# Three of the weights' low parts subtracted on GpSimd instead of being made by TensorE

## The chip, the cores and the metric

The kernel runs on one core of a Trainium2 chip. Its engines are TensorE (PE, with its weight loads shown as PEld), VectorE (DVE), ScalarE (ACT), GpSimd (POOL) and SyncE (SP), which issues the loads and stores. The metric is the device time of one execution in microseconds, the median of several runs.

## What is computed

The reference has two halves. The first is attention with local and global keys, for 4 batches of 8 heads, 768 positions and head dimension 64; the second is a channel mix of the result with its predecessor in the sequence:

```python
scores = scale * q @ k.T + bias        # bias = -slope(head) * distance
scores = where(is_global | is_local, scores, -1e9)   # 8 global keys, 96 local
x = softmax(scores) @ v                # then [B, S, 512]
x_prev = concatenate([0, x[:, :-1]], axis=1)
xk = mu_k * x + (1 - mu_k) * x_prev
xr = mu_r * x + (1 - mu_r) * x_prev
k = maximum(xk @ w_k, 0)               # w_k [512, 1024]
v = k * k @ w_v                        # w_v [1024, 512]
out = sigmoid(xr @ w_r) * v            # w_r [512, 512]
```

The three weights come as 64-bit floats.

## The kernel before

The 4 x 768 positions are cut into 24 tiles of 128. For every tile and pair of heads PE makes the scores (`s_n_hp`, lines 357 and 358 in the first eight tiles), DVE adds the bias and takes the maximum (L366), ACT exponentiates (L367), DVE takes the reciprocal of the sum (`r_n_hp`, L373 and L374), and of each four heads three are scaled by `r` on POOL (L380) and one on ACT (L378). PE transposes the scaled heads (`t_n_hp`, L392), ACT copies them out of PSUM (`et`), and PE multiplies them by the values (`av_n`, L411). A scaled head is called `e_n_h`.

Two tiles make a chunk of 256 positions for the channel mix. `mix` makes `xk` and `xr` (L435 or L437 for the predecessor's part, L438 on DVE) and cuts each into a high part on ACT (L439, type fp32r) and a low part on DVE (L440, `xk_lo` and `xr_lo`). Each product is then three matmuls: high by high, high by low, low by high (L447 to L449). `kp` are the products of `xk` with w_k, `z` those of `xr` with w_r, `vps` those of the square with w_v. In the `kp` products the weight is the stationary operand: line 447 is its high part by `xk_hi`, line 448 its high part by `xk_lo`, line 449 its low part by `xk_hi`.

The weights are cut the same way. They lie in DRAM as 64-bit words and come in ten blocks of 1 MB: 0 to 3 are w_k (`wk0` to `wk3`), 4 and 5 are w_r (`wr0`, `wr1`), 6 to 9 are w_v (`wv0` to `wv3`). A block's words land in `w64_i`. `weight_begin` makes a 32-bit float `wa_i` of them in three steps on DVE (L174, L175, L176) and its high part on ACT (L178). `weight_end` makes the low part: for w_k and w_r through PE, which puts `wa` times the identity less the high part into a PSUM tile `rest` (L188 and L189, in two halves of 512 columns; L188 is a product of 32-bit floats and has two records in the trace for each instruction), from which ACT casts it (L190); for w_v directly on DVE by a subtraction of 128 x 1024 (L192).

W_BEGUN says at which point of the program a block is begun; it is ended one such point later. A scheduler that times the program by its own estimates then sets the order in which the instructions of all engines stand; each engine works through its own list in that order and waits for what the instruction at its head needs. The conversion of the weights, the first tiles' attention and the first chunk's `kp` lie in the first 100 us; afterwards the weights stay in SBUF.

Of the kernel before, what the change touches and what calls it, by code (L numbers as in the profile page):

```python
# [9 lines left out]
F32 = mybir.dt.float32  # L10
# [22 lines left out]

W_LOADS = (2, 2, 2, 2, 3, 3, 4, 4, 4, 5, 5, 6, 6, 7, 7, 8, 8, 9, 9, 10)
W_BEGUN = (1, 1, 2, 2, 3, 3, 4, 4, 4, 5, 5, 6, 6, 6, 7, 7, 8, 8, 9, 9, 10)
GAP = {"kk_hi": 16, "xk_lo": 112}
FAR = 1.0e12
HUGE = (1.875 - 2.0**-13) * 2.0**32
# [3 lines left out]
def tile_biased_attention_channel_mix(ctx: ExitStack, tc: tile.TileContext, qT, kT, v, n_sizes, mu_kr, w_k, w_v, w_r, q_rows, k_rows, v_rows, slopes, out):  # L42
    nc = tc.nc
    vec, act, pool, pe = nc.vector, nc.scalar, nc.gpsimd, nc.tensor
# [57 lines left out]
    f_pool.tile([128, 96], F32, name="ahead", tag="ahead")  # L102
    btmp = f_pool.tile([128, 2048 + GAP["kk_hi"]], F32, name="btmp", tag="kk_hi")
    cut = iter((0, 352, 704, 928, 1056, 1184, 1184 + W))
# [77 lines left out]
    def weight_end(i):  # L182
        name, src, j = w_steps[i]
        a, both = w_live.pop(i)
        if name in 'kr':
            for o in (0, 512):
                rest = ps_f.tile([128, 512], F32, name=f"rest_{i}_{o}", tag="f")
                pe.matmul(rest, ident, a.bitcast(F32)[:, o : o + 512], start=True, stop=False)  # L188
                pe.matmul(rest, minus, both[:, 0, o : o + 512], start=False, stop=True)  # L189
                act.copy(both[:, 1, o : o + 512], rest)  # L190
        else:
            vec.tensor_sub(both[:, 1, :], a.bitcast(F32), both[:, 0, :])  # L192
        for k in range(1 if name == "k" else 2):
            kn = both if name == "k" else both[:, :, k * 512 : (k + 1) * 512]
            wts[name, j if name == "k" else 2 * j + k] = kn[:, 0, :], kn[:, 1, :]
# [41 lines left out]
    def weights_load(n):  # L237
        while w_count[2] < min(n, len(w_steps)):
            weight_load(w_count[2])
            w_count[2] += 1  # L240

    def weights_go(begun, ended):
        weights_load(begun)
        while w_count[0] < min(begun, len(w_steps)):
            weight_begin(w_count[0])
            w_count[0] += 1
        while w_count[1] < min(ended, w_count[0]):
            weight_end(w_count[1])
            w_count[1] += 1
# [175 lines left out]
    def part(pool, tag, n):  # L425
        t = pool.tile([128, n * 256 + GAP.get(tag, 0)], F32R, name=tag, tag=tag)
        return t[:, 0 : n * 256].rearrange("p (a q) -> p a q", a=n)
# [97 lines left out]
    for step in range(NTILES + 1):  # L525
# [6 lines left out]
        for hp in range(4):  # L532
# [19 lines left out]
            weights_load(W_LOADS[min(slot, len(W_LOADS) - 1)])  # L552
            n = W_BEGUN[min(slot, len(W_BEGUN) - 1)]
            weights_go(n, n - 1 if slot < len(W_BEGUN) else n)
    for i in range(4):
# [190 lines left out]
```

## Time and profile before

| | |
|---|---|
| median of 3 runs | 509.49 us (509.43 to 509.81) |
| the profiled execution | 509.01 us, its span 507.2 us |
| busy in the span | PE 98%, DVE 68%, ACT 68%, POOL 44% |
| granted TensorE clock, mean | 0.996 of full speed |
| waits of PE after 20 us | 1.2 us, the first L448 for `xk_lo` |

The profile is of one execution; the span runs from its first to its last instruction, and 1.8 us lie around it. The busy shares are means over the whole span, and what holds in the first 100 us, where the change is, is read from the windows and timelines of that stretch.

### The profile page before, as it was taken

How to read it: one execution, taken by the hardware profiler on the slowest of the kernel's cores; microseconds unless marked ns; L12 is line 12 of the kernel's file. 1: busy time of each engine (PE TensorE's matmuls, PEld its weight loads, DVE VectorE, ACT ScalarE, POOL GpSimd, SP SyncE). 2: the span in 40 equal slices, each digit the busy share in tenths (PEclk: the TensorE clock that was granted, in tenths of full speed). 3: DMA queues.
4: the chain of work that ended last, by engine and by line, in shares of the span. 5: the costliest groups of instructions: out<-in, count | busy, mean ns of one | idle time of the engine just before them, and what ended most of it. 6: DMA issues, size and time to landing. Idle time of an engine off the chain costs nothing. (4 is left out here: it accounts for less than half of the span.)

```text
span 507.2 us, 10304 instructions
## 1 busy us (share of the span) xinstructions
PE 495.6 (98%) x3600; PEld 434.4 (86%) x3600; DVE 342.9 (68%) x837; ACT 345.0 (68%) x857; POOL 221.5 (44%) x368
## 2 busy tenths in 40 slices
PE   6999999999999999999999999999999999999995
PEld 3767898998898898898898898898898898897984
DVE  6986988466388768658768758748768755457441
ACT  4889789567467668667577677667577678587360
POOL 8631435224448445527447536428438435204000
PEclk9999999999999999999999999999999999999999
DMA  8998331503913433513513513513423215647311
GB/s 242 323 241 241 137 111 51 151 1 101 209 34 80 107 100 79 151 55 80 142 46 81 149 57 80 142 64 79 124 66 81 82 40 163 208 156 258 126 41 48
DMA packets 24234, 59.95 MB, mean 118 GB/s; under 512 B 5328, under 2 KB 6352, under 8 KB 23664
## 3 DMA queue, kind: packets, MB, share of 16 engines
q1 hardware_dynamic: 24032, 59.23, 40.6%
q8 instruction: 30, 0.49, 0.4%
q14 instruction: 28, 0.23, 0.2%
q10 hardware_dynamic: 144, 0.00, 0.0%
HBM read 52.93 MB, written 6.29 MB: 117 GB/s over the span
## 5 line engine op out<-in xcount | busy, mean ns | idle before, releaser
L380 POOL TENSOR_SCALAR e<-e,r 128x232 f32<-128x232 f32 (+1 forms) x180 | 89.2, 514 | 162.2 <-DVE r L374 125.4
L447 PE MATMUL kp<-xk_hi,wk 128*128 128x256 f32 x384 | 108.8, 283 | 0.0
L448 PE MATMUL kp<-xk_lo,wk 128*128 128x256 f32 x384 | 107.5, 280 | 1.2 <-DVE xk_lo L440 1.2
L367 ACT ACTIVATE e<-e,nmax 128x232 f32<-128x232 f32 (+1 forms) x192 | 89.9, 471 | 26.5 <-DVE nmax L366 25.8
L449 PE MATMUL kp<-xk_hi,wk 128*128 128x256 f32 x384 | 107.5, 280 | 0.0
L366 DVE CUSTOM_DVE_ANT_0 e<-s,pat 128x232 f32<-128x232 f32 (+1 forms) x192 | 64.7, 373 | 25.2 <-PE s L361 14.0
L447 PE MATMUL vps<-wv,kk_hi 128*128 128x512 f32 x192 | 75.6, 395 | 0.0
L449 PE MATMUL vps<-wv,kk_lo 128*128 128x512 f32 x192 | 75.2, 392 | 0.0
L448 PE MATMUL vps<-wv,kk_hi 128*128 128x512 f32 x192 | 75.0, 391 | 0.0
L448 PEld LDWEIGHTS kp<-xk_lo,wk 128*128 128x128 f32 x384 | 72.1, 188 | 2.0 <-DVE xk_lo L440 1.4
L447 PEld LDWEIGHTS kp<-xk_hi,wk 128*128 128x128 f32 x384 | 72.2, 188 | 0.4
L449 PEld LDWEIGHTS kp<-xk_hi,wk 128*128 128x128 f32 x384 | 72.1, 188 | 0.1
L394 ACT COPY et<-t 128x256 f32<-128x256 f32 (+1 forms) x176 | 56.7, 373 | 10.2 <-PE t L392 9.6
L475 DVE TENSOR_TENSOR kk<-kp,kk 128x512 f32<-128x512 f32 x48 | 33.0, 688 | 41.6 <-ACT kk L474 41.3
L392 PE MATMUL t<-ident,e 128*128 128x128 f32 x352 | 55.4, 277 | 0.2 <-ACT et L394 0.2
L477 DVE TENSOR_TENSOR kk_lo<-kk,kk_hi 128x512 fp32r<-128x512 f32 x48 | 35.0, 730 | 22.6 <-ACT kk_hi L476 22.2
L392 PEld LDWEIGHTS t<-ident,e 128*128 128x128 f32 x352 | 40.7, 136 | 10.9 <-issue 2.3
L449 PEld LDWEIGHTS vps<-wv,kk_lo 128*128 128x128 f32 x192 | 36.0, 188 | 7.8
L447 PEld LDWEIGHTS vps<-wv,kk_hi 128*128 128x128 f32 x192 | 36.1, 188 | 6.8 <-issue 0.2
L448 PEld LDWEIGHTS vps<-wv,kk_hi 128*128 128x128 f32 x192 | 36.2, 188 | 6.6
L476 ACT CAST kk_hi<-kk 128x512 fp32r<-128x512 f32 x48 | 29.9, 622 | 16.8 <-DVE kk L475 16.8
L411 PE MATMUL av<-et,va 128*64 128x128 f32 x384 | 40.4, 282 | 0.0
(113 smaller groups left out, 1079.6 us busy)
## 6 DMA issues: line engine op xcount, KB each, us to landing
qraw<-in_qT_dram SPq DMA_DIRECT2D x32, 256.0 KB
kraw<-in_kT_dram SPq DMA_DIRECT2D x32, 256.0 KB
out_dram<-sig SPq DMA_DIRECT2D x24, 256.0 KB
va<-in_v_dram SPq DMA_DIRECT2D x20, 240.0 KB
vb<-in_v_dram SPq DMA_DIRECT2D x20, 208.0 KB
w<-in_w_k_dram SPq DMA_DIRECT2D x4, 1024.0 KB
w<-in_w_v_dram SPq DMA_DIRECT2D x4, 1024.0 KB
again<-in_w_k_dram SPq DMA_DIRECT2D x8, 512.0 KB
```

The lines of the kernel that those rows point to most:

```text
L366: vec.tensor_tensor_reduce(out=e[:, :w], in0=o, in1=p[:, h, :], op0=ALU.add, op1=ALU.min, scale=-0.125, scalar=3.0e38, accum_out=s["nmax"] ...
L367: act.activation(e[:, :w], e[:, :w], AF.Exp, bias=s["nmax"][:, h : h + 1], scale=-1.0, accum_out=s["sum"][:, h : h + 1])
L380: pool.tensor_scalar(e[:, :w], e[:, :w], r[:, u : u + 1], 1.0, op0=ALU.mult, op1=ALU.mult)
L392: pe.transpose(pt[0:p, c : c + 128], e[:, k * 128 : k * 128 + p], ident)
L394: act.copy(et[0:p, k * 256 : k * 256 + 256], pt[0:p, k * 256 : k * 256 + 256])
L411: pe.matmul(o, vt[:, h * 64 : (h + 1) * 64], et[0:p, c + q : c + 128], start=k == 0, stop=k == nb - 1)
L447: pe.matmul(o, sh, mh, start=first, stop=False)
L448: pe.matmul(o, sh, ml, start=False, stop=False)
L449: pe.matmul(o, sl, mh, start=False, stop=last)
L475: vec.tensor_mul(kk, pv, kk)
L476: high = act.copy(kkh[:, 2 * fp : 2 * fp + 2, :], kk)
L477: rest = vec.tensor_sub(kkl[:, 2 * fp : 2 * fp + 2, :], kk, kkh[:, 2 * fp : 2 * fp + 2, :])
```

## The change

A string says for each of the ten blocks which engine makes its low part: P is TensorE with ScalarE as before, G is GpSimd, D is VectorE. Blocks 0 to 2 stay on TensorE, block 3 of w_k and both blocks of w_r go to GpSimd, w_v's four stay on VectorE.

```diff
 W_BEGUN = (1, 1, 2, 2, 3, 3, 4, 4, 4, 5, 5, 6, 6, 6, 7, 7, 8, 8, 9, 9, 10)
+LOW = "PPPGGGDDDD"
...
-        if name in 'kr':
+        if LOW[i] == "P":
             for o in (0, 512):
                 rest = ps_f.tile([128, 512], F32, name=f"rest_{i}_{o}", tag="f")
                 pe.matmul(rest, ident, a.bitcast(F32)[:, o : o + 512], start=True, stop=False)
                 pe.matmul(rest, minus, both[:, 0, o : o + 512], start=False, stop=True)
                 act.copy(both[:, 1, o : o + 512], rest)
         else:
-            vec.tensor_sub(both[:, 1, :], a.bitcast(F32), both[:, 0, :])
+            (pool if LOW[i] == "G" else vec).tensor_sub(both[:, 1, :], a.bitcast(F32), both[:, 0, :])
```

Line numbers from there on are one higher in the new kernel. The scheduler sets a new order for the first 100 us. In the rows below, as in the trace, a name carries the tile's number and then the head or the pair, and a running number at its end. In POOL's list there stood, behind the scaled heads of tile 2 and before those of tile 3:

```order
L380 TENSOR_SCALAR e_2_3_449<-e_2_3_449,r_2_1_452 128x232
L255 TENSOR_SCALAR x_1_735<-x_0_406 128x4
L380 TENSOR_SCALAR e_2_5_493<-e_2_5_493,r_2_3_515 128x232
L380 TENSOR_SCALAR e_2_6_509<-e_2_6_509,r_2_3_515 128x232
L380 TENSOR_SCALAR e_2_7_512<-e_2_7_512,r_2_3_515 128x232
L255 TENSOR_SCALAR kz_0_179<-k_first_188 64x8x8
L380 TENSOR_SCALAR e_3_1_580<-e_3_1_580,r_3_1_628 128x232
```

and there stand now, with the three subtractions (L193) among them:

```order
L381 TENSOR_SCALAR e_2_3_449<-e_2_3_449,r_2_1_452 128x232
L193 TENSOR_TENSOR wk3_361<-wa_3_357,wk3_361 128x1024
L256 TENSOR_SCALAR x_1_714<-x_0_406 128x4
L381 TENSOR_SCALAR e_2_5_486<-e_2_5_486,r_2_3_508 128x232
L381 TENSOR_SCALAR e_2_6_502<-e_2_6_502,r_2_3_508 128x232
L381 TENSOR_SCALAR e_2_7_505<-e_2_7_505,r_2_3_508 128x232
L193 TENSOR_TENSOR wr0_467<-wa_4_463,wr0_467 128x1024
L256 TENSOR_SCALAR kz_0_179<-k_first_188 64x8x8
L193 TENSOR_TENSOR wr1_521<-wa_5_517,wr1_521 128x1024
L381 TENSOR_SCALAR e_3_1_566<-e_3_1_566,r_3_1_614 128x232
```

The subtraction of `wk3` stands behind `e_2_3`, and those of `wr0` and `wr1` behind `e_2_7`, ahead of the heads of tile 3.

DVE's list had `xk_lo` right behind the first step of block 7, with the heads of tile 3 around it:

```order
L175 SCALAR_TENSOR_TENSOR wa_6_658<-w64_6_637,wa_6_658 128x1024
L176 SCALAR_TENSOR_TENSOR wa_6_658<-w64_6_637,wa_6_658 128x1024
L174 TENSOR_SCALAR wa_7_798<-w64_7_713 128x1024
L440 TENSOR_TENSOR xk_lo_585<-mix_k_583,xk_hi_584 128x1024
L366 ISA e_3_6_685,nmax_3_460<-s_3_3_680,pat_136 128x232
```

It now has the first heads of tile 4 and the further steps of blocks 6 and 7 ahead of it, and `r_3_1` stands among these:

```order
L176 SCALAR_TENSOR_TENSOR wa_6_644<-w64_6_623,wa_6_644 128x1024
L375 RECIPROCAL r_3_1_614<-r_3_1_614 128x4
L175 TENSOR_SCALAR wa_7_777<-w64_7_692 128x1024
L177 SCALAR_TENSOR_TENSOR wa_6_644<-w64_6_623,wa_6_644 128x1024
L176 SCALAR_TENSOR_TENSOR wa_7_777<-w64_7_692,wa_7_777 128x1024
L441 TENSOR_TENSOR xk_lo_571<-mix_k_569,xk_hi_570 128x1024
L374 TENSOR_SCALAR r_3_3_670<-sum_3_459 128x4
L177 SCALAR_TENSOR_TENSOR wa_7_777<-w64_7_692,wa_7_777 128x1024
```

`xk_lo` (now L441) has moved behind two more long steps, the last of block 6 and the second of block 7. Behind it stands the last step of block 7.

PE's list had, around the first product with `xk_lo`, the last of `av_2`, one pair of heads and one L447:

```order
L411 MATMUL av_2_718<-et_2_1_610,vb_2_410 64x104
L357 MATMUL s_4_0_751<-kz_0_179,qz_0_178 128x104
L358 MATMUL s_4_0_751<-kz_1_183,qz_0_178 128x128
L357 MATMUL s_4_0_751<-kz_0_179,qz_0_178 128x104
L358 MATMUL s_4_0_751<-kz_1_183,qz_0_178 128x128
L447 MATMUL kp_700<-xk_hi_584,wk0_215 128x256
L448 MATMUL kp_700<-xk_lo_585,wk0_215 128x256
L449 MATMUL kp_700<-xk_hi_584,wk0_215 128x256
```

Now the eight transposes of the first four heads of tile 3 are the last work ahead of it, with three L447 (now L448) ahead of them; the rows begin within these transposes:

```order
L393 MATMUL t_3_0_722<-ident_62,e_3_1_566 128x128
L393 MATMUL t_3_0_722<-ident_62,e_3_1_566 104x128
L393 MATMUL t_3_1_784<-ident_62,e_3_2_608 128x128
L393 MATMUL t_3_1_784<-ident_62,e_3_2_608 104x128
L393 MATMUL t_3_1_784<-ident_62,e_3_3_611 128x128
L393 MATMUL t_3_1_784<-ident_62,e_3_3_611 104x128
L449 MATMUL kp_679<-xk_lo_571,wk0_215 128x256
L450 MATMUL kp_679<-xk_hi_570,wk0_215 128x256
```

The last eight `av_2` and the pairs `s_4_1` and `s_4_2`, which stood behind the first L448 before, stand ahead of these transposes now. The list of SP's loads and stores is in the same order as before.

## Rows read from the trace of the kernel before

**Rows 1.** Page, busy time: engine, us, share of the span, instructions

```profile
PE 495.6 (98%) x3600; PEld 434.4 (86%) x3600; DVE 342.9 (68%) x837; ACT 345.0 (68%) x857; POOL 221.5 (44%) x368
```

**Rows 2.** Waits of PE: line, waited for, us, times, longest

```profile
PE kp L448 <- DVE xk_lo L440: 1.2, 1, 1.2
```

**Rows 3.** Windows: length, busy PE, PEld, DVE, ACT, POOL, PEclk, DMA, GB/s

```profile
45.00:50.00 5.00, 5.00 (x33) 2.96 (x32) 3.69 (x7) 3.98 (x12) 0.00 (x0) 1.00 0.73 191
50.00:55.00 5.00, 3.84 (x32) 3.52 (x30) 4.89 (x13) 4.08 (x13) 0.00 (x0) 1.00 0.01 2
```

**Rows 4.** Timeline of PE: start us, us, instruction [idle before and releaser]

```profile
44.13 1.02 PE L188 MATMUL rest<-wa,ident 128*128 128x512 f32 x2
...
45.31 0.43 PE L411 MATMUL av<-et,va 128*64 128x128 f32 x2
...
50.47 0.36 PE L447 MATMUL kp<-xk_hi,wk 128*128 128x256 f32 x1
51.99 0.39 PE L448 MATMUL kp<-xk_lo,wk 128*128 128x256 f32 x1 [1.16 <-DVE xk_lo L440]
52.22 0.28 PE L449 MATMUL kp<-xk_hi,wk 128*128 128x256 f32 x1
52.34 0.28 PE L447 MATMUL kp<-xk_hi,wk 128*128 128x256 f32 x1
```

**Rows 5.** Lines by form, PE, 17 to 60 us: count, busy us, mean ns

```profile
L188 PE MATMUL rest<-wa,ident 128*128 128x512 f32 x24 | 12.5, 610 | 0.0
```

**Rows 6.** Timeline of DVE between 34 and 52 us

```profile
34.61 0.71 DVE L174 TENSOR_SCALAR wa<-w 128x1024 int32<-128x1024 int32 x1 [1.58 <-DMA w<-in_w_r_dram]
...
39.16 0.39 DVE L366 CUSTOM_DVE_ANT_0 e<-s,pat 128x232 f32<-128x232 f32 x1
39.48 1.87 DVE L438 SCALAR_TENSOR_TENSOR mix_k<-x,mus,mix_k 128x256 f32<-128x256 f32 x4
...
47.66 1.23 DVE L176 SCALAR_TENSOR_TENSOR wa<-w,wa 128x1024 int32<-128x1024 int32 x1
50.11 0.69 DVE L174 TENSOR_SCALAR wa<-w 128x1024 int32<-128x1024 int32 x1 [1.23 <-DMA w<-in_w_v_dram]
50.72 1.22 DVE L440 TENSOR_TENSOR xk_lo<-mix_k,xk_hi 128x1024 fp32r<-128x1024 f32 x1
```

**Rows 7.** Lines by form, POOL: the one-input copy of 128x1024

```profile
L255 POOL TENSOR_SCALAR qh<-qraw 128x1024 fp32r<-128x1024 f32 x16 | 16.9, 1056 | 21.9 <-PE s L360 20.2 <-PE s L358 1.7
```

**Rows 8.** Timelines of DVE and POOL between 173 and 177 us

```profile
173.98 2.05 DVE L336 TENSOR_TENSOR ql<-qraw,qh 128x1024 fp32r<-128x1024 f32 x1 [1.73 <-POOL qh L255]
...
173.91 1.05 POOL L255 TENSOR_SCALAR kw<-kraw 128x1024 fp32r<-128x1024 f32 x1
```

**Rows 9.** Timeline of POOL, and line 380's durations (min/median/max ns)

```profile
32.09 2.15 POOL L380 TENSOR_SCALAR e<-e,r 128x232 f32<-128x232 f32 x3 [2.64 <-ACT et L394]
...
55.81 2.79 POOL L380 TENSOR_SCALAR e<-e,r 128x232 f32<-128x232 f32 x3 [11.19 <-DVE r L374]
...
L380 POOL TENSOR_SCALAR e<-e,r x180: 370/462/1589, 11.7 to 440.9; 128x232 f32<-128x232 f32 x150, 128x128 f32<-128x128 f32 x30
```

**Rows 10.** Timeline of PE: `kp` products on both sides of interrupting work

```profile
54.81 0.28 PE L447 MATMUL kp<-xk_hi,wk 128*128 128x256 f32 x1
...
56.87 0.28 PE L447 MATMUL kp<-xk_hi,wk 128*128 128x256 f32 x1
...
58.52 0.28 PE L449 MATMUL kp<-xk_hi,wk 128*128 128x256 f32 x1
...
59.65 0.28 PE L448 MATMUL kp<-xk_lo,wk 128*128 128x256 f32 x1
...
62.00 0.28 PE L447 MATMUL kp<-xk_hi,wk 128*128 128x256 f32 x1
...
63.11 0.28 PE L449 MATMUL kp<-xk_hi,wk 128*128 128x256 f32 x1
```

**Rows 11.** Windows, the columns of rows 3

```profile
10.00:20.00 10.00, 9.30 (x63) 7.68 (x62) 8.16 (x30) 8.53 (x33) 4.72 (x9) 0.83 1.04 329
```

## Prediction

> **What bounds the kernel now.** Read the busy shares first: PE works 98% of the span [rows 1], so the time is PE's work plus its few waits. The waits of PE come next: after the start-up only one is over half a microsecond, the 1.2 us of the first `kp` matmul of line 448 for `xk_lo` [rows 2]. The windows show the same thing: PE is full up to 50 us, and in 50 to 55 us it has 3.84 of 5 while POOL has nothing at all [rows 3]. PE's timeline says where: the first product L447 starts at 50.47, the second, L448, not before 51.99 [rows 4]. From there PE has almost no hole until the end. So one number carries the forecast: **when the first L448 can start, and how much PE work stands ahead of it**. Whatever PE saves ahead of that point is lost in waiting, unless later work is drawn ahead of it.
>
> **What is removed.** Half of the 24 records of L188 [rows 5] and as many L189 of the two later weight groups go: six `rest` tiles. One of them holds PE from 44.13 to 45.31, so 1.18 us [rows 4], and six come to 7.1 us. All six stand ahead of the first L448. If that start could move freely the gain would be 7.1 us and the time 502.4. It can't: `xk_lo` comes from DVE, and behind DVE stand the weights' DMAs. Before, `xk_lo` (50.72) waits only for L174 of w7, which starts at 50.11 when w7 lands, 1.23 us after DVE had run dry [rows 6]. ACT also loses six casts; it isn't waited for at this place, so I put these at nothing.
>
> **What is moved on DVE.** In the new order `xk_lo` stands behind L174 of w7 and two more long steps, L176 of w6 and L175 of w7. Start to start, L174 costs 0.61 (50.11 to 50.72), and an L175 or L176 1.15 (its 1.23 less the 0.08 that L174 overlaps its follower by) [rows 6]. So without any disturbance `xk_lo` ends at 50.11 + 0.61 + 2 x 1.15 + 1.22 = 54.24, against 51.94 before: **2.3 us later**. The DMA that sets the 50.11 I leave where it is. Its issue waits for PE's `av`, which may come one `rest` tile, 1.2 us, earlier; as the queue is busy with other loads until then I count none of it, and all of it is the end of the range in A below.
>
> **What is drawn ahead on PE.** Between the old and the new place of the first L448 stand now: the last eight `av_2` matmuls, heads `s_4_1` and `s_4_2`, eight transposes of `t_3_0` and `t_3_1`, and two more L447. From rows in which each interrupts a run of `kp` (spaced 0.12 [rows 4]): `av_2` 54.81 to 56.87 less three `kp`, 1.71; `s_4_1` 58.52 to 59.65 less two, 0.89, and the same for `s_4_2`; the transposes 62.00 to 63.11 less two, 0.87; two L447 0.24 [rows 10]. Sum: **4.6 us** that PE no longer does behind the gate. With 2.3 later and 4.6 less to do, the undisturbed result is a gain of 2.3 us.
>
> **What is added on POOL.** Three subtractions of 128x1024 with two inputs. No row shows POOL doing one. The shortest they can be is POOL's copy of one input of that size, 1.06 us [rows 7]; I take two passes of it, 2.11, since a second input must also be read, and since DVE pays about double as well (L440 1.22 against L174's 0.61 [rows 6]). For the upper end I take three passes, 3.2. The Trainium skill, "GPSIMD Engine Reference", section 3.1, gives 4497 ns for an elementwise add of 2048 and keeps such work on VectorE; an estimate from it for 1024 is 2.25 us, which would put 0.4 us on the sum below (three times 0.14). No run so far shows it.
>
> POOL is idle for long stretches here (11.19 us ahead of 55.81 [rows 9]), so its own time would be free. But it isn't alone: at 173.98 DVE starts the subtraction `ql`, 0.07 us behind a POOL copy that runs 173.91 to 174.96, and it takes 2.05 us where the same size takes 1.22 undisturbed. It has been **held until POOL was through** and then done whole [rows 6, 8]. The other way round POOL's L380 takes 462 ns in the median and up to 1589 [rows 9]. This is what the Trainium skill says ("SBUF — State Buffer", section "Who interferes with whom"): GpSimd and a VectorE instruction with two SBUF inputs share one port pair, and whichever is first keeps it for its whole instruction. The trace agrees with it in the 2.05 us.
>
> **The sum with the holds.** DVE's work in the new order from 34.61 (L174 of w5) to the end of `xk_lo`: three L174 at 0.61, six L175/L176 at 1.15, ten L366 at 0.32, four L438 together 1.79 (1.87 less an overlap of 0.08), L440 1.22: 14.9 us [rows 6]. The short ones L373 and L374 are left out. Without a break it would end at 49.5, so the two DMA landings leave DVE 54.24 - 49.5 = 4.7 us of slack. Three subtractions of 2.11 meet it: the first starts when POOL has finished its three L380 (32.09 + 2.15 = 34.24 [rows 9]) and holds L174 from 34.61 to about 36.3, 1.7 us; the other two fall among L176, L438 and L174 and can cost 1.9 each, the length less about 0.2 as in the 2.05 us above. Together 5.5: the slack is gone, and `xk_lo` ends at 49.5 + 5.5 = 55.0.
>
> Now POOL itself: r for `e_3_1` to `e_3_3` leaves DVE 4.1 us ahead of that end (L174, L176, L175, L440), at 50.9. POOL then has to scale three heads, on which the transposes wait that now stand ahead of the first L448. But DVE runs five long steps without a gap until L176 of w7 ends at 56.2. Both engines want the same port, so two orders bound it. If POOL gets in between each time, the three L380 (0.46 each) push `xk_lo` to 56.4. If POOL always comes last, `e_3_3` is ready at 56.2 + 1.4 = 57.6, and two transposes (0.11 each) and a signal later L448 starts at 57.9. In the one place of the trace where three L380 meet such a run they take 2.79 us instead of 1.4 [rows 9], which is nearer the former; but there the DVE steps were the short L438 for the most part. I take the middle, and 0.1 for the short steps left out: **57.3**. That is 5.3 later than 51.99, less the 4.6: **+0.7 us**, with 56.4 and 57.9 as ends -0.2 and +1.3.
>
> The profiled execution took 509.01 us (span 507.2 and 1.8 around it), the median of the runs is 509.49, 0.5 above it. I apply the difference to the median: 509.49 + 0.7 = **510.2**. 0.2% is 1.0 us and about what a measurement of this kernel can tell from no change.
>
> **The rivals.**
> A. *The holds cost nothing.* The subtraction is short, or DVE isn't held by it. For it: DVE has 4.7 us of slack, so holds of up to 1.5 each vanish, which is a subtraction of about 1.7 us. Against it: the 2.05 us of [rows 8]. Then the gate is 54.3 and the result -2.3: 507.2, faster; with the load 1.2 us earlier 506.0, of which I give little.
> B. *The subtraction is long.* At three passes (3.2 us) each hold grows by 1.1, the gate by 3.3: +4.0, so 513.5; at 2.6 us +2.2, so 511.7. It decides from about 2.2 us, where the sum passes +1.0. For it: POOL's two-input rate is the one price that no row gives. Slower.
> C. *PE's clock.* PE now stands idle for some 9 us (the 7.1 removed, the 5.3 of the later gate and the 1.2 of before, less the 4.6 drawn ahead) between 34 and 57 us. In 10 to 20 us, behind the waits of the start-up, its granted clock was 0.83 in the mean, so the lower of the levels 1.2 and 2.4 GHz for part of it [rows 11]: 0.17 x 10 is 1.7 us that it cost. If that comes back once, the sum is +0.7 + 1.7: 511.9, slower. Against it: the hole of 1.2 us at 51 us left it at 1.00 [rows 3], and the new holes are spread out.
> D. *Nothing reaches the end.* A wait behind the gate (the fourth `kp` for its PSUM slot, `z` for `xr_lo`) gives PE's 4.6 us back: then the loss is up to the whole 5.3 us of the later gate, half of the 4.6 lost being +3.0, 512.5. For it: DVE's steps behind `xk_lo` are as late as `xk_lo`. Against: PE has 69 `kp` matmuls, 8 us, straight behind the gate.
>
> **How the numbers follow.** The sum above 0.45 (its own range 509.3 to 510.8; of its 0.45 I put 0.29 inside 0.2%, 0.15 above, since the gate's upper end passes it, and 0.01 below), A 0.27, B 0.12, C 0.10, D 0.06. Faster is A and the sum's lower edge, 0.28; within 0.2% is most of the sum, 0.29; slower is B, C, D and the upper part of the sum, 0.43. The likeliest single case is the sum, 510.2. The range reaches from A, 507.1, to the middle of B and C, 512.4.
>
> **What will show it.** Right: the three POOL subtractions at 2.0 to 2.3 us; an L174 or L175 and two of the L438 or L176 at about 3 us instead of 1.2 or less; the slowest step ahead of the first L448 being a transpose that waits for POOL's `e_3_3`; that L448 at 56.4 to 57.9. Wrong: DVE rows that keep their lengths beside POOL's subtraction (A); subtractions over 2.6 us (B); a granted clock under 1.00 between 40 and 65 us (C); PE waits of over 0.5 us between 60 and 80 us (D).

## The result, and the profile after

The new kernel takes 512.62 us in the median of five runs (512.40 to 513.52) against 509.49: it is slower by 0.6%, the ratio is 1.0062 with an interval of 1.0045 to 1.0079. The profiled execution took 512.40 us, its span 510.6. The forecast was 510.2 in a range of 507.1 to 512.4, so the time lies just outside it, on the side that had the largest chance.

Nearly all of it happens before 80 us. The first `vps` product starts at 78.18 in the trace of before and at 81.29 in that of after, 3.1 us later; from 80 us on the two run in parallel but for 0.4 us near 150 us, where PE waits 0.2 us for DVE that it didn't wait for before. Line numbers of after are one higher than those of before.

The page's busy line of after; PE is busy for 3.5 us less than in [rows 1], and the span is 3.4 us longer all the same:

```profile
PE 492.1 (96%) x3582; PEld 434.0 (85%) x3582; DVE 349.8 (69%) x837; ACT 342.0 (67%) x851; POOL 231.9 (45%) x371
```

PE's waits (columns as in [rows 2]). The wait for `xk_lo` is gone from the list; other waits stand in its place, and the longest is ahead of a pair of heads:

```profile
PE s L358 <- issue: 3.5, 1, 3.5
PE t L393 <- POOL e L381: 2.4, 2, 1.3
PE s L358 <- DVE nmax L367: 1.3, 1, 1.3
```

The windows of the stretch, the columns of [rows 3]. PE has 1.52 of 5 us to do in 45 to 50 us, half the clock for a good part of 50 to 55, and 2.62 of 5 in 55 to 60, while DVE is full throughout:

```profile
45.00:50.00 5.00, 1.52 (x15) 1.22 (x14) 5.00 (x11) 1.16 (x5) 2.81 (x3) 1.00 0.87 173
50.00:55.00 5.00, 5.00 (x38) 4.72 (x37) 5.00 (x13) 3.78 (x13) 2.13 (x2) 0.66 0.03 11
55.00:60.00 5.00, 2.62 (x21) 2.12 (x21) 5.00 (x14) 4.50 (x11) 4.88 (x5) 1.00 0.74 210
```

POOL's timeline shows the new subtractions (L193) and the scaled heads of tile 3 (the first three of the six L381 at 52.87):

```profile
33.25 2.59 POOL L381 TENSOR_SCALAR e<-e,r 128x232 f32<-128x232 f32 x3 [2.73 <-ACT et L395]
35.81 3.34 POOL L193 TENSOR_TENSOR wk<-wa,wk 128x1024 fp32r<-128x1024 f32 x1
...
41.78 3.34 POOL L193 TENSOR_TENSOR wr<-wa,wr 128x1024 fp32r<-128x1024 f32 x1
...
45.48 2.33 POOL L193 TENSOR_TENSOR wr<-wa,wr 128x1024 fp32r<-128x1024 f32 x1
52.87 7.02 POOL L381 TENSOR_SCALAR e<-e,r 128x232 f32<-128x232 f32 x6 [5.06 <-DVE r L375]
```

A subtraction takes 2.33 us when nothing is ahead of it (45.48). The other two took 3.34, and DVE's timeline says why: the first starts at 35.81 while L177 is running (35.50 to 36.91), so POOL waits 1.0 and then works 2.33.

```profile
35.50 1.41 DVE L177 SCALAR_TENSOR_TENSOR wa<-w,wa 128x1024 int32<-128x1024 int32 x1
36.83 3.40 DVE L176 SCALAR_TENSOR_TENSOR wa<-w,wa 128x1024 int32<-128x1024 int32 x1
...
42.81 5.68 DVE L439 SCALAR_TENSOR_TENSOR mix_k<-x,mus,mix_k 128x256 f32<-128x256 f32 x3
...
48.73 0.39 DVE L367 CUSTOM_DVE_ANT_0 e<-s,pat 128x232 f32<-128x232 f32 x1
...
54.33 1.39 DVE L176 SCALAR_TENSOR_TENSOR wa<-w,wa 128x1024 int32<-128x1024 int32 x1
55.65 1.21 DVE L441 TENSOR_TENSOR xk_lo<-mix_k,xk_hi 128x1024 fp32r<-128x1024 f32 x1
```

And L176, which follows at 36.83, waits for POOL in turn: 3.40 us instead of 1.22. The three L439 at 42.81 take 5.68 instead of the 1.27 that they take in run 1 below, with two subtractions among them. PE's wait of 3.5 us ends at 49.23, 0.1 us behind the L367 with which DVE goes on after them (48.73 to 49.12); the page names no releaser for it, so that the link to the held L439 is inferred. `xk_lo` (L441) ends at 56.86.

PE's timeline at the gate, the rows that answer to [rows 4]:

```profile
55.21 0.60 PE L393 MATMUL t<-ident,e 128*128 128x128 f32 x4
57.16 0.44 PE L393 MATMUL t<-ident,e 128*128 128x128 f32 x2 [1.35 <-POOL e L381]
58.63 0.44 PE L393 MATMUL t<-ident,e 128*128 128x128 f32 x2 [1.03 <-POOL e L381]
58.82 0.36 PE L449 MATMUL kp<-xk_lo,wk 128*128 128x256 f32 x1
```

The first product with `xk_lo` starts at 58.82, 6.83 us later than before, and not for `xk_lo`: the transposes ahead of it wait twice for POOL's heads.

### The profile page after: what moved, and what is told of

Same layout as the page of the kernel before. It is cut to its first block, busy times and chain, and to the rows that moved or that the text cites. A ratio compares the mean times of both kernels' runs of the same rounds, so it can differ in the third digit from the quotient of the medians.

```text
span 510.6 us, 10269 instructions
## 1 busy us (share of the span) xinstructions
PE 492.1 (96%) x3582; PEld 434.0 (85%) x3582; DVE 349.8 (69%) x837; ACT 342.0 (67%) x851; POOL 231.9 (45%) x371
## 5 line engine op out<-in xcount | busy, mean ns | idle before, releaser
L381 POOL TENSOR_SCALAR e<-e,r 128x232 f32<-128x232 f32 (+1 forms) x180 | 91.5, 527 | 168.5 <-DVE r L375 131.7
L448 PE MATMUL kp<-xk_hi,wk 128*128 128x256 f32 x384 | 108.4, 283 | 0.0
L367 DVE CUSTOM_DVE_ANT_0 e<-s,pat 128x232 f32<-128x232 f32 (+1 forms) x192 | 64.6, 373 | 26.2 <-PE s L362 14.0
L448 PE MATMUL vps<-wv,kk_hi 128*128 128x512 f32 x192 | 75.6, 395 | 0.0
L448 PEld LDWEIGHTS kp<-xk_hi,wk 128*128 128x128 f32 x384 | 72.0, 188 | 0.8 <-issue 0.2
L448 PEld LDWEIGHTS vps<-wv,kk_hi 128*128 128x128 f32 x192 | 36.2, 188 | 6.8 <-issue 0.2
```

Source lines behind the costliest of these rows:

```text
L367: vec.tensor_tensor_reduce(out=e[:, :w], in0=o, in1=p[:, h, :], op0=ALU.add, op1=ALU.min, scale=-0.125, scalar=3.0e38, accum_out=s["nmax"] ...
L381: pool.tensor_scalar(e[:, :w], e[:, :w], r[:, u : u + 1], 1.0, op0=ALU.mult, op1=ALU.mult)
L448: pe.matmul(o, sh, mh, start=first, stop=False)
```

## The experiments

Each time is compared with runs of the kernel before that were taken with it; their median was 509.3 for the first eight and 509.7 for the last four, so medians from different sets can be compared to a few tenths at best. "The gate" is the first product with `xk_lo`, at 51.99 in the trace of before and at 58.82 in that of after.

| | gate, us | median, us | ratio to before |
|---|---|---|---|
| the new kernel | 58.82 | 512.62 | 1.0062 (1.0045 to 1.0079) |
| 1, no subtraction | 54.60 | 509.80 | 1.0014 (1.0003 to 1.0025) |
| 2, copy in its place | 54.26 | 510.20 | 1.0019 (1.0007 to 1.0031) |
| 3, all three on DVE | 57.87 | 513.25 | 1.0078 (1.0054 to 1.0102) |
| 4, heads of tile 3 on ACT | 57.40 | 512.06 | 1.0058 (1.0041 to 1.0076) |
| 5, kernel before, `xk_lo` first | 50.60 | 508.94 | 0.9980 (0.9960 to 1.0001) |
| 6, new kernel, `xk_lo` first | 51.07 | 507.20 | 0.9965 (0.9943 to 0.9986) |
| 7, w_r on POOL, `xk_lo` first | 52.12 | 508.31 | 0.9971 (0.9950 to 0.9991) |
| 8, all on DVE, `xk_lo` first | 48.88 | 504.90 | 0.9896 (0.9848 to 0.9943) |
| 9, as 1, PE kept busy | 54.50 | 507.02 | 0.9947 (0.9924 to 0.9969) |
| 10, only w_r on POOL | 53.83 | 509.65 | 1.0007 (0.9982 to 1.0032) |
| 11, only block 3 on POOL | 53.81 | 508.61 | 0.9980 (0.9963 to 0.9998) |
| 12, block 3 on DVE, w_r on POOL, `xk_lo` first | 51.05 | 505.96 | 0.9919 (0.9891 to 0.9948) |

**1. The subtraction taken away.** The high part is used again where the low one belongs; the order of every engine is that of the new kernel.

```diff
-        else:
-            (pool if LOW[i] == "G" else vec).tensor_sub(both[:, 1, :], a.bitcast(F32), both[:, 0, :])
+        elif LOW[i] == "D":
+            vec.tensor_sub(both[:, 1, :], a.bitcast(F32), both[:, 0, :])
...
-            wts[name, j if name == "k" else 2 * j + k] = kn[:, 0, :], kn[:, 1, :]
+            wts[name, j if name == "k" else 2 * j + k] = kn[:, 0, :], kn[:, 0 if LOW[i] == "G" else 1, :]
```

> The new kernel in the same order on every engine, but the three subtractions on POOL are left out (the high part is used again where the low part of blocks 3 to 5 belongs). Port theory (POOL's subtractions hold DVE, DVE's run holds POOL): DVE's L176 and L177 keep about 1.2 us, xk_lo ends at 54.2 when block 7 lands at 50.1, and since the scaled heads of tile 3 are ready well ahead of that, the first product with xk_lo starts at 54.3 instead of 58.8; total 4.5 us less than the new kernel, about 508.1. Order rival (xk_lo behind block 7 and the changed list on PE are what costs, the subtraction is free): it stays at 58 and 512.5. Clock rival (the half clock at 50 to 54 us is what costs): PE is still idle ahead of 54 us, so the half clock should come back and the time stay over 510.5.

DVE's three L439 take 1.27 us here:

```profile
41.14 1.27 DVE L439 SCALAR_TENSOR_TENSOR mix_k<-x,mus,mix_k 128x256 f32<-128x256 f32 x3
```

The gate came where the port theory put it, at 54.60, and it waits for `xk_lo` alone. Yet the time is 509.80 instead of 508.1. The clock rival is right in that the half clock came back, though not in its time of over 510.5. PE's timeline around the gate and, behind it, two neighbours in the run of `kp`:

```profile
54.60 0.39 PE L449 MATMUL kp<-xk_lo,wk 128*128 128x256 f32 x1 [4.14 <-DVE xk_lo L441]
...
55.17 0.41 PE L450 MATMUL kp<-xk_hi,wk 128*128 128x256 f32 x1
55.38 0.41 PE L448 MATMUL kp<-xk_hi,wk 128*128 128x256 f32 x1
```

They come 0.21 us apart instead of 0.12, and the windows show the granted clock of 0.66 in 55 to 60 us, behind a hole in which PE had 0.86 of 5 us to do:

```profile
50.00:55.00 5.00, 0.86 (x8) 0.61 (x6) 4.56 (x6) 1.47 (x3) 0.00 (x0) 1.00 0.91 247
55.00:60.00 5.00, 5.00 (x31) 5.00 (x31) 5.00 (x15) 5.00 (x17) 1.32 (x3) 0.66 0.71 283
```

0.34 of 5 us is 1.7 us. So 2.8 us of the new kernel's loss are the subtraction on POOL (2.4 by the ratios), and even without it the order gains nothing.

**9. The same, with PE kept busy in the hole.** Sixteen products of zeros go into a PSUM tile that the first real product overwrites (`warm` is 16 in the first chunk, else 0).

```diff
             ps = ps_f.tile([128, 512], F32, name="kp", tag="f")
+            if warm and fp == 2:
+                for i in range(warm):
+                    pe.matmul(ps, zeros[:, 0:128], zeros, start=True, stop=True)
```

> As the run without the three subtractions, but 16 products of zeros (3.5 us at full clock) stand on PE behind the first three L448 of kp, in the hole of 4.1 us ahead of the first product with xk_lo; nothing else is changed ahead of it. Clock theory (there the gate came at 54.6 and the gain of the work drawn ahead was eaten by PE running at half clock from 55.1 to 58.3, products at 0.21 us instead of 0.12): the gate stays at 54.3 to 54.8, the products behind it come at 0.12 us at once, and the time falls by 1.5 us against that run, to 508.0 to 508.5. If the clock is not what costs: 509.8.

The gate is where it was, and the clock stays up:

```profile
49.22 3.63 PE L467 MATMUL kp<-zeros 128*128 128x512 bf16 x16
...
54.50 0.38 PE L449 MATMUL kp<-xk_lo,wk 128*128 128x256 f32 x1 [0.66 <-DVE xk_lo L441]
...
55.19 0.28 PE L448 MATMUL kp<-xk_hi,wk 128*128 128x256 f32 x1
55.31 0.28 PE L449 MATMUL kp<-xk_lo,wk 128*128 128x256 f32 x1
```

```profile
55.00:60.00 5.00, 5.00 (x44) 5.00 (x44) 5.00 (x16) 5.00 (x16) 2.70 (x3) 1.00 0.58 223
```

The time fell by 2.8 us against run 1 (3.4 by the ratios), more than the 1.5 expected. PE's list differs from run 1 behind the gate too: in run 1, as in the new kernel, `av_3` stands in three pieces among `kp` and `z`, here its matmuls run without a break. The traces tell the two apart. From the gate to the first `vps` PE has the same instructions to do in run 1, in the new kernel and in run 9, and takes 24.01, 22.47 and 21.63 us. Run 1 and the new kernel have the same list there, but only run 1 has the half clock: 1.5 us. The new kernel and run 9 both have the full clock, but different lists: 0.8 us. Against the trace of before, run 9 has its gate 2.51 us later and its first `vps` 2.05 us earlier (76.13): 4.6 us of work were drawn ahead, the sum of the prediction.

**2. A copy in place of the subtraction.** POOL reads one input instead of two (the low parts are the whole weights). PE, DVE and ACT have the new kernel's order; in POOL's list, other than expected below, the copies of `wk3` and `wr0` stand each ahead of three heads of tile 2 instead of behind them.

```diff
-            (pool if LOW[i] == "G" else vec).tensor_sub(both[:, 1, :], a.bitcast(F32), both[:, 0, :])
+            if LOW[i] == "G":
+                pool_copy(both[:, 1, :], a.bitcast(F32))
+            else:
+                vec.tensor_sub(both[:, 1, :], a.bitcast(F32), both[:, 0, :])
```

> The new kernel with a copy of one input (1.06 us where it is undisturbed) in place of each subtraction, so the low parts are wrong; same order everywhere. Port theory: the holds are now 3 x 1.1 = 3.3 us, less than the 4.7 us that DVE has in hand before block 7 lands, so the result lies within 0.5 us of the run without any subtraction, about 508.2 to 508.6. A theory in which any extra POOL work at this place costs in proportion: half of the loss stays, about 510.5.

Within 0.4 us of run 1, as the port theory had it, though both stand at least 1.6 us over the numbers given: PE again waits long ahead of the gate, and behind it the granted clock is 0.78 in 55 to 60 us.

```profile
54.26 0.58 PE L452 MATMUL kp<-xk_lo,wk 128*128 128x256 f32 x1 [3.38 <-DVE xk_lo L444]
```

On DVE only one hold of some length is left: the three steps of `mix_k` take 2.45 us instead of 1.27. The copy of `wr0` (39.11 to 40.15) meets two L370 there, and they keep their 0.40 us.

```profile
41.75 2.45 DVE L442 SCALAR_TENSOR_TENSOR mix_k<-x,mus,mix_k 128x256 f32<-128x256 f32 x3
```

This vanishes in DVE's slack; 6.6 us of holds in the new kernel don't. So it is not enough that POOL does something at this place. Whether the length, the second input or the place in POOL's list makes the difference isn't separated by this run.

**4. The heads of tile 3 on ACT.** One more term in the condition: `if n < 6 and u < 1 or n == 3 and hp == 1`.

> The new kernel with heads 1 to 3 of tile 3 scaled on ACT instead of POOL; PE's list then has the first product with xk_lo ahead of the transposes of tile 3. If the last two microseconds at the gate are POOL's scaling held off by DVE's run, the first product with xk_lo starts with the end of xk_lo, at 56.9 to 57.0, and as 0.9 us of transposes are no longer drawn ahead the total is about 1 us under the new kernel, 511.6. If the gate was xk_lo itself or PE's clock, nothing moves: 512.6.

```profile
57.40 0.38 PE L449 MATMUL kp<-xk_lo,wk 128*128 128x256 f32 x1 [1.15 <-DVE xk_lo L441]
```

The gate now waits for `xk_lo`, and comes 1.4 us earlier than in the new kernel, not 1.8 to 1.9: `xk_lo` itself ended 0.5 us later, at 57.34. PE was at half clock from 47 to 54 us here (the granted clock is 0.73 in 45 to 50 and 0.59 in 50 to 55), and DVE waited for its scores:

```profile
51.41 0.40 DVE L367 CUSTOM_DVE_ANT_0 e<-s,pat 128x232 f32<-128x232 f32 x1 [0.58 <-PE s L359]
```

So POOL's scaling, kept waiting by DVE's run of long steps, was the last part of the new kernel's gate. What it costs in the end isn't settled: the total fell by 0.6 us and not by 1.0, and the intervals of the two ratios overlap.

**3. The three subtractions on DVE.** `LOW = "PPPDDDDDDD"`.

> The same three low parts subtracted on DVE (1.15 us each) instead of POOL. Port theory: DVE's own 3.5 us fit into its 4.7 us of slack, nothing is held; xk_lo ends at 53.7 to 54.3, the first product with it starts 1.8 to 2.3 us later than in the kernel before, and less work is drawn ahead of it (four av_2, s_4_1, t_3_0, t_3_1, two products: about 2.3 us): 509.0, within 0.2% of before. Order rival: like the new kernel, 512.

A clear miss: 513.25, 1.2 us over the order rival's 512. Nothing is held by POOL's subtraction, for there is none. But `r` of tile 3 now stands behind block 7's landing, and POOL's three L381 then meet DVE's run:

```profile
53.03 4.45 POOL L381 TENSOR_SCALAR e<-e,r 128x232 f32<-128x232 f32 x3 [10.13 <-DVE r L375]
```

4.45 us where they need 1.4. PE waits for them ahead of every transpose, after a first wait of 4.81 us for ACT's head:

```profile
53.50 0.69 PE L393 MATMUL t<-ident,e 128*128 128x128 f32 x2 [4.81 <-ACT e L379]
...
57.53 0.69 PE L393 MATMUL t<-ident,e 128*128 128x128 f32 x2 [0.78 <-POOL e L381]
57.87 0.56 PE L449 MATMUL kp<-xk_lo,wk 128*128 128x256 f32 x1
```

```profile
50.00:55.00 5.00, 1.10 (x4) 0.53 (x4) 4.06 (x9) 0.96 (x3) 1.97 (x2) 0.54 0.97 284
55.00:60.00 5.00, 3.44 (x16) 2.74 (x15) 5.00 (x12) 4.31 (x11) 2.50 (x3) 0.50 0.48 190
```

and runs at half clock for nearly ten microseconds. So the same gate is late with no subtraction on POOL at all: the port holds both ways, and what it holds up depends on the order.

**10 and 11. One part alone.** `LOW = "PPPPGGDDDD"` and `LOW = "PPPGPPDDDD"`, in the scheduler's own orders.

> Only the two blocks of w_r on POOL, block 3 on PE as before, in the scheduler's own order, in which xk_lo stands behind the first step of block 7 alone and the scaled heads of tile 3 are not ahead of the gate. Gate theory: two holds of 2.2 us take up DVE's slack, xk_lo ends at 52.0 to 52.6 and the first product with it starts at most 0.6 us later than in the kernel before, with 0.9 us or more drawn ahead of it: 508.5 to 509.5. Port theory alone (each subtraction on POOL costs about 1 us): 511.3.

> Only block 3 of w_k on POOL, both blocks of w_r on PE as before, in the scheduler's own order: xk_lo behind the first step of block 7 and two L367. One hold of 2.2 us, within DVE's slack. Gate theory: xk_lo ends at 52.6, 0.7 us later than in the kernel before, with 1.8 us drawn ahead (s_4_1, s_4_2): 508.3 to 508.8. Port theory alone: 510.3.

Run 11's median lies in the span given by the gate theory, run 10's 0.15 us above it; both are well under the port theory's numbers. The gates are later than expected. In run 11 PE gets there only then, without a wait, with more work drawn ahead:

```profile
53.81 0.39 PE L449 MATMUL kp<-xk_lo,wk 128*128 128x256 f32 x1
```

In run 10 the profiled execution (512.1 us) is 2.5 us longer than the median, so its gate of 53.83 need not be that of a usual run. In it block 7 landed at 51.9, 1.8 us later than in [rows 6], for a cause that stays open; PE then waited 2.37 us at the gate, and the granted clock behind it is 0.78 in 55 to 60 us:

```profile
51.88 0.69 DVE L175 TENSOR_SCALAR wa<-w 128x1024 int32<-128x1024 int32 x1 [1.40 <-DMA w<-in_w_v_dram]
```

```profile
53.83 0.58 PE L449 MATMUL kp<-xk_lo,wk 128*128 128x256 f32 x1 [2.37 <-DVE xk_lo L441]
```

Either part alone, in the order that goes with it, costs nothing that these runs can tell from zero: there one or two holds fit into DVE's slack, and of block 7's steps only the first stands ahead of `xk_lo`. In the new kernel the three holds meet an order in which more stands ahead of `xk_lo` and of the gate. Holds of DVE are not needed for a late gate: run 3 is late without one, by its order.

**5, 6, 7, 8 and 12. `xk_lo` ahead of block 7.** The first of a block's steps on DVE is issued behind `xk_lo` of the first chunk, for block 7 in run 5 and for blocks 6 and 7 in the others, where block 6 is also begun two points later.

```diff
-W_BEGUN = (1, 1, 2, 2, 3, 3, 4, 4, 4, 5, 5, 6, 6, 6, 7, 7, 8, 8, 9, 9, 10)
+W_BEGUN = (1, 1, 2, 2, 3, 3, 4, 4, 4, 5, 5, 6, 6, 6, 6, 6, 8, 8, 9, 9, 10)
...
-        vec.tensor_scalar(a, top, 3, 0x3FFFFFF8, op0=ALU.logical_shift_left, op1=ALU.bitwise_and)
+        with tc.issue_after(first_lo[0].ins) if i >= 6 else ExitStack():
+            vec.tensor_scalar(a, top, 3, 0x3FFFFFF8, op0=ALU.logical_shift_left, op1=ALU.bitwise_and)
...
-        vec.tensor_sub(lo, tmp, hi)
+        first_lo.append(vec.tensor_sub(lo, tmp, hi))
```

Run 5, with `LOW = "PPPPPPDDDD"` and only block 7 behind `xk_lo`:

> All low parts made as in the kernel before; only DVE's first step of block 7 is issued behind xk_lo instead of ahead of it. Gate theory (the one thing that the saved work of PE runs into is xk_lo, and xk_lo waits for block 7's landing): PE's wait of 1.2 us at the first product with xk_lo goes, 508.0 to 508.3. Rival (PE's total work sets the time and the wait is made up elsewhere): 509.3.

```profile
50.60 0.28 PE L451 MATMUL kp<-xk_lo,wk 128*128 128x256 f32 x1
```

PE's wait is gone and in the profiled execution the gate is 1.4 us earlier. The median is 0.3 us under that of before, the interval 0.9960 to 1.0001: it points the right way, but 508.94 lies outside the 508.0 to 508.3 expected, and the gain of 1 us isn't settled by it.

Run 6, the new kernel's `LOW`:

> The new kernel's three subtractions on POOL, but the steps of blocks 6 and 7 on DVE are issued behind xk_lo. The holds of DVE by POOL stay (three of 2.2 us). Gate theory: xk_lo ends near 52 instead of 56.9 and POOL's scaling of tile 3 no longer meets DVE's run ahead of the gate; the first product with xk_lo then waits for PE's own order and starts at 54 to 55 instead of 58.8; 509 to 510, so 2.5 to 3.5 us under the new kernel. Rival (the holds alone cost the 3 us): 512 to 512.6.

DVE's timeline:

```profile
48.56 1.23 DVE L443 TENSOR_TENSOR xk_lo<-mix_k,xk_hi 128x1024 fp32r<-128x1024 f32 x1 [0.17 <-ACT xk_hi L442]
...
50.79 2.81 DVE L177 TENSOR_SCALAR wa<-w 128x1024 int32<-128x1024 int32 x1 [0.37 <-DMA w<-in_w_v_dram]
```

The same three subtractions on the same engine, and 5.4 us less than the new kernel, 2 us more than expected: `xk_lo` ends at 49.79, not near 52, and the gate comes 3 us ahead of the 54 to 55 given. POOL's third subtraction now holds the first step of block 7 (L177 in this kernel, 2.81 us instead of 0.69) behind it, where it delays nothing at the gate.

Run 7, `LOW = "PPPPGGDDDD"`:

> Only the two blocks of w_r on POOL, block 3 stays on PE, and the steps of blocks 6 and 7 on DVE behind xk_lo. PE loses 4.7 us of work ahead of the gate; two holds of 2.2 us; xk_lo ends near 48.5, PE gets there at about 46.6, so the first product with xk_lo starts at 48.6, 3.4 us earlier than in the kernel before, with 0.9 us drawn ahead: 505 to 506 if the hole of 2 us leaves PE's clock up, 506 to 507 if it halves it for a while. Port rival (DVE and POOL stay so entangled that xk_lo comes as late as before): 509.

```profile
44.24 0.47 PE L360 MATMUL s<-kz,qz 128*128 128x104 f32 x2 [1.96 <-DVE nmax L369]
```

```profile
45.00:50.00 5.00, 5.00 (x33) 3.54 (x32) 4.71 (x14) 4.56 (x18) 2.93 (x3) 0.66 0.79 219
```

Faster than before, but 1.3 us over the 506 to 507 given for a halved clock: PE waited 1.96 us at 44.24 for DVE, which POOL's two subtractions held, and then ran at half clock; the mean of 0.66 over 5 us is 1.7 us. DVE's rows:

```profile
39.95 3.60 DVE L441 SCALAR_TENSOR_TENSOR mix_k<-x,mus,mix_k 128x256 f32<-128x256 f32 x3
43.48 0.39 DVE L369 CUSTOM_DVE_ANT_0 e<-s,pat 128x232 f32<-128x232 f32 x1
```

The gate came at 52.12, 3.5 us later than expected, and PE was at work ahead of it.

Run 8, `LOW = "PPPDDDDDDD"`:

> The three low parts on DVE, nothing added on POOL, and the steps of blocks 6 and 7 on DVE behind xk_lo. No holds; DVE does 3 x 1.15 us more, xk_lo ends near 48, the first product with it starts at 48 to 49: 505 to 506. If the port was what spoiled the change and not the order, this equals the run with the three subtractions on DVE in the scheduler's order, 513.

504.90, a tenth under the 505 to 506 expected, with the gate at 48.88 as expected: 4.4 us under the kernel before and 8.4 under run 3, which has the same low parts on DVE and differs in that order alone. It beats both kernels. Run 12, `LOW = "PPPDGGDDDD"` in the same order:

> Block 3 on DVE, the two blocks of w_r on POOL, and the steps of blocks 6 and 7 on DVE behind xk_lo: between the run with all three on POOL in that order (507.2) and the one with all three on DVE (504.9). If each POOL subtraction costs about 0.8 us there, 506.4; if only the one of block 3 costs, 505.

505.96, between the two numbers expected: two subtractions on POOL cost 1.1 us against DVE, three 2.3 us (run 6). The intervals of the ratios of runs 8 and 12 overlap and the orders differ a little too, so that this isn't the price of the port alone.

## Why the prediction was right or wrong, point by point

The mechanism was foretold and two terms of its sum were mis-sized. The gate with the holds was taken at 57.3 and came at 58.82, 1.5 us later, because POOL's subtractions held DVE for longer than counted. The work drawn ahead was taken as 4.6 us and 3.7 arrived, 0.9 us less, because the list behind the gate had not been read. Either alone would have left the time inside the range (511.7 or 511.1); both together did not.

- **The gate** (right as the place, too early with the holds). Nearly all that moved the time was the start of the first product with `xk_lo` and the work that stands ahead of it. Undisturbed it was put at 54.3, and runs 1, 2 and 9 have it at 54.60, 54.26 and 54.50.
- **POOL's subtraction** (mis-sized). Taken as 2.11, it is 2.33, and that is without the wait for DVE that may precede it. The prediction's estimate of 2.25, half of the 4497 ns that the Trainium skill ("GPSIMD Engine Reference", section 3.1) gives for an add of 2048, was nearer; the trace is 0.08 above it.
- **The holds** (mechanism right, size wrong; the larger of the two failed terms). Taken as 5.5 us in all, they are 2.2 for L176 and 4.4 for the L439, so 6.6, with a few tenths more on L177 and L176 and on the short steps that were left out. The first was put at 1.7 because POOL was expected to be at it from 34.24; its three heads started 1.2 us later (33.25 against 32.09 in [rows 9]), so the whole subtraction fell on DVE's run. `xk_lo` ended at 56.9, not at 55.0.
- **POOL's heads behind DVE's run** (right). The transposes did wait, and 58.82 is 2.0 us behind the end of `xk_lo`; the middle that was taken gives 2.3. The three L381 took 1.79, 2.47 and 1.49 us instead of 0.46 each: by DVE's rows the second was passed over by two long steps, L176 and `xk_lo`. Run 4 took it away.
- **The work drawn ahead** (the other term that failed). 4.6 us were counted and 3.7 arrived: gate 6.83 later, first `vps` 3.11 later. The count of what stood ahead was right (run 9 has 4.6). What was missed is the list behind the gate. `av_3`, one run of 1.80 us in the trace of before, stands in three pieces in the new order; they begin at 68.89, 72.68 and 77.56 in the rows below and cost 0.76, 0.55 and 0.95 us up to the next instruction, 2.26 together. Against run 9, which has the same instructions behind its gate in another order, the new kernel's 0.84 us are 0.46 for `av_3`, 0.34 for the heads `s` and a few hundredths for the rest. Only the order up to the gate had been read, not that of the next twenty microseconds.

The one run in the trace of before, and what follows it:

```profile
73.60 0.45 PE L411 MATMUL av<-et,va 128*64 128x128 f32 x4
...
75.40 0.66 PE L392 MATMUL t<-ident,e 128*128 128x128 f32 x4
```

The three pieces in the new kernel, with what follows the first two:

```profile
68.89 0.45 PE L412 MATMUL av<-et,va 128*64 128x128 f32 x4
...
69.66 0.39 PE L448 MATMUL kp<-xk_hi,wk 128*128 128x256 f32 x1
...
72.68 0.30 PE L412 MATMUL av<-et,vb 104*64 104x104 f32 x1
...
73.23 0.50 PE L448 MATMUL z<-wr,xr_hi 128*128 128x512 f32 x1
...
77.56 0.30 PE L412 MATMUL av<-et,vb 104*64 104x104 f32 x1
```

- **The sum.** +0.7 becomes +0.7 + 1.5 (gate at 58.8 instead of 57.3) + 0.9 (drawn ahead) = +3.1, the difference of the traces at 81 us; 0.4 more near 150 us came from a place that the prediction didn't look at.
- **Rival A** would have been 507.2. Without the holds it is 509.8 (run 1), since A left out the half clock behind the gate and the list of PE there. With the clock kept up and `av_3` in one piece, it is 507.0 (run 9).
- **Rival C, the clock** (underrated, and put at the wrong place). In the new kernel it fell to half from 50 to 54 us, after the wait of 3.5 us at 49.2, but PE waited 2.4 us for POOL behind that and ahead of the gate, more than the clock cost, so by the rows nothing of it reaches the end (not tried by itself). In run 1 it fell behind the gate and cost 1.5 to 1.7 us. That, with the list, is the flaw in the prediction's "undisturbed" gain of 2.3 us: the hole ahead of the gate brought the half clock behind it.
- **Rival B** (513.5) and **rival D** (512.5) lie nearer to 512.62 than the forecast, as C's 511.9 does, but that is luck. B's condition was met, 2.33 us being over its 2.2, yet by the prediction's sum that length gives +1.4 and not +3.1. D did not occur: PE has no wait of over 0.2 us between 60 and 80 us, and the 0.9 us of drawn work were lost without one.

## What to carry to other kernels

When a change takes work off the bounding engine, find the first thing behind it that comes from elsewhere, and move that first: here the same three subtractions cost 3.1 us in one order and gained 2 in another. Read the new order not only up to the gate but as far as it differs, since work that is drawn ahead is only won if what is left behind stays in one piece. Long two-input steps on POOL beside a full VectorE were paid on VectorE here: three of 2.33 us held it for 6.6 us, and this reached the result as soon as VectorE's idle time was used up.

## What the runs showed of the hardware that was not expected

- The hold works both ways in one chain: POOL's subtraction waited 1.0 us for the DVE step that was running, and the next DVE step waited 2.2 us for POOL (35.81 and 36.83). A single-input step is held as well: the L177 of run 6, 2.81 us instead of 0.69.
- Not every DVE step is held. In run 7 POOL's second subtraction runs from 43.20 to 45.79. The two L369 within it (43.48 and 43.79), which read the scores from PSUM, keep their 0.39 us each, and the step of `mix_k` behind them at 44.11 takes 1.96 us instead of 0.48. So the price of a subtraction on POOL hangs on which DVE steps it meets.
- PE's granted clock fell to half, 1.2 GHz, in or behind holes of 3.5 us (the new kernel), 4.1 (run 1), 4.8 (run 3) and 2.4 (run 10), and in run 7 behind one of 1.96. In run 10 a hole of the same 1.96 us, ahead of 44.4, left it at 1.00, so the length of the last hole alone doesn't tell. It came back with steady work; in run 3, where PE went on waiting between transposes, only after 60 us. Products of zeros kept it up (run 9).
